# Decode attention over a KV cache: eight value blocks sent as 112 + 8 + 8 partitions instead of 128

## The chip, the cores and the metric

The kernel runs on one core of one Trainium2 chip. The metric is the device time of one execution in microseconds. Runs of the kernel before mostly agree within 0.3%. Times inside a profile count from the first instruction of the profiled run (its "span", 1 to 3 us shorter than the measured time).

## The reference, cut to what matters

Two attention layers decode one token for four sequences; A attends to all 8192 keys, B to the last 2048.

```python
def _A_ref(x, k_cache, v_cache, wq, wo):     # B=4, Sq=1, D=512, Hq=32, Hkv=8, Sk=8192, Dh=128, bf16
    q = (x @ wq) ...                         # per head
    scores = einsum("bhqd,bhkd->bhqk", q, k) * Dh ** -0.5
    p = softmax(scores)
    o = einsum("bhqk,bhkd->bhqd", p, v)
    return o ... @ wo
# B is the same on k_cache[:, :, Sk - 2048:], v_cache[:, :, Sk - 2048:]
# ... (result: concatenate A and B)
```

All of it is reading: 184.56 MB come from HBM, and every cached key and value is used once.

## The kernel before

Work is cut into 40 units: 8 of pass B, then 32 of pass A, one for each sequence and KV head. A unit of A has a key block and a value block of 2 MB each. Partition p holds 64 consecutive keys, so one block is 128 rows of 16 KB, one row to a partition.

```python
    def kv_src(cache, u, q=None):
        ...
            ap = cache[un["b"], un["g0"]].rearrange("(p t) d -> p t d", p=128)
    ...
        K_sb = sb("K_sb", [128, NKS, NT, DH], BF16)      # NKS = 3 slots
        V_sb = sb("V_sb", [128, NVS, NT, DH], BF16)      # NVS = 4 slots
    ...
        def sp_V(u):
            waits = [("PV", (u - NVS) * NQ + NQ - 1)] if u >= NVS else []
            # ... (last unit: four column quarters; pass B: two halves of the columns)
            else:
                op("sp", dma(kv_dst(V_sb, u % NVS, u), kv_src(VC[units[u]["P"]], u)), waits=waits, inc=("V", u))
```

SyncE issues one key and one value block per unit as slots come free. TensorE transposes the keys (L308 in the profile), forms the scores (L339) and multiplies probabilities by values (L365, the consumer of the changed transfers).

## Time and profile before

| | before |
|---|---|
| time, median of the runs | 454.71 us (453.95 to 455.2, four runs) |
| HBM bytes, rate over the span | 184.56 MB, 408 GB/s |
| TensorE busy | 370.2 of 452.4 us |
| 16 KB row on one DMA engine | 0.613 us |
| 16 KB rows over 0.7 us, after 119 us of the span | 45 of 7936 |

From the page of the kernel before, the lines of the 40 slices for DMA (busy tenths) and for GB/s, and two queues with packets, MB and share of 16 engines' time.

```profile
DMA  8999999999999999999999999999999999999971
GB/s 354 397 412 419 445 404 423 415 419 423 409 421 423 430 420 431 420 427 424 426 426 426 424 429 422 430 419 430 422 429 423 427 425 424 424 425 424 427 325 77
...
q1 hardware_dynamic: 17040, 184.56, 97.1%
q8 instruction: 53, 0.87, 0.8%
```

The DMA engines are busy nearly all the time, and from 150 us of the span to near its end they move about 425 GB/s. Queue q1 carries the tensors. Queue q8 is the fetching of instructions: few bytes.

The chain that ended last, from the same page, with shares of the span:

```profile
## 4 chain that ended last, share of the span: by engine, by line
DMA 54%; PE 38%; issue 3%; DVE 2%; ACT 1%; POOL 0%; POOLq 0%
DMA K_sb<-in_A_k_cache_dram 30%; PE ps L308 20%; DMA V_sb<-in_A_v_cache_dram 18%; DMA W<-in_A_wq_dram 6%; PE ps L365 6%; PE ps L339 5%; PE ps L438 3%; PE ps L254 2%; ACT KT_sb L317 1%; PE ps L728 1%; DVE KT_sb L316 1%; DVE M L456 1%; DVE Dt L494 0%; DVE xo_sb L553 0%; ACT PT L505 0%
```

The list of waits, before: who waited for whom, total us, times, longest.

```profile
...
PE ps L308 <- DMA K_sb<-in_A_k_cache_dram: 30.0, 19, 10.1
...
PE ps L365 <- DMA V_sb<-in_A_v_cache_dram: 9.0, 8, 2.3
...
```

TensorE waits for keys more than for values, in short gaps.

DMA issues, before: KB each, and the median time from issue to landing in us.

```profile
K_sb<-in_A_k_cache_dram SPq DMA_DIRECT2D x32, 2048.0 KB, 21.9
V_sb<-in_A_v_cache_dram SPq DMA_DIRECT2D x31, 2048.0 KB, 26.9
...
```

A block takes 8 x 0.613 = 4.9 us at the full rate, so 22 to 27 us from issue to landing means that about five blocks are queued.

The trace also holds every DMA packet, without the number of its engine. I chained each packet's end to the start that follows within a few ns, which rebuilds 16 engines (neighbours with equal times can be swapped in this, so I use it for groups, not for single engines over long times). About half of them land their last row near 436 us of the span, one at 440 us, the rest at 444.5 to 446 us. A fetch and the row behind it take 2.16 us, so a fetch costs its engine 2.16 - 0.61 = 1.55 us, and 53 fetches over eight engines are 53 x 1.55 / 8 = 10.3 us each. That is the skew the change aims at. That the fetches run on just eight engines is inferred from this sum and from their order, since the trace does not name the engines.

### The profile page before, as it was taken

The page shows a single profiled execution, that of the slowest core. Times are in us where ns is not written, and L with a number is a line of the kernel's source. Part 1 is how long each engine was busy: PE and PEld are TensorE (multiplying, and loading weights), DVE is VectorE, ACT ScalarE, POOL GpSimd, SP SyncE. Part 2 cuts the span into 40 slices and gives each one's busy share as a digit, 9 for nine tenths or more (in the row PEclk, how much of TensorE's full clock was granted, in tenths as well). Part 3 has the DMA queues.
Part 4 walks back from the last instruction along what each step waited for, and adds up shares of the span by engine and source line. Part 5 has one row for each costly group of instructions (what it writes and reads, how often), then busy time and mean ns, then how long its engine had stood idle before and what let it go on. Part 6 is the DMA issues. An engine that isn't in the chain of part 4 may idle for free.

```text
span 452.4 us, 14605 instructions
## 1 busy us (share of the span) xinstructions
PE 370.2 (82%) x6793; PEld 340.0 (75%) x6793; DVE 195.1 (43%) x449; ACT 178.0 (39%) x202; POOL 35.8 (8%) x93
## 2 busy tenths in 40 slices
PE   0682279999919998989978898878989789988997
PEld 0682279968818797888878888777979788888796
DVE  0351225748604453434434453444445344444362
ACT  1150214525503362534334453433444343345270
POOL 1100000100100110000000010001001000010010
PEclk9996655889958985968878896978868795698697
DMA  8999999999999999999999999999999999999971
GB/s 354 397 412 419 445 404 423 415 419 423 409 421 423 430 420 431 420 427 424 426 426 426 424 429 422 430 419 430 422 429 423 427 425 424 424 425 424 427 325 77
DMA packets 17181, 185.51 MB, mean 410 GB/s; under 512 B 1744, under 2 KB 2272, under 8 KB 4704
## 3 DMA queue, kind: packets, MB, share of 16 engines
q1 hardware_dynamic: 17040, 184.56, 97.1%
q8 instruction: 53, 0.87, 0.8%
q14 instruction: 8, 0.07, 0.0%
q0 software_dynamic: 64, 0.01, 0.0%
q10 hardware_dynamic: 16, 0.01, 0.0%
HBM read 184.56 MB, written 0.01 MB: 408 GB/s over the span
## 4 chain that ended last, share of the span: by engine, by line
DMA 54%; PE 38%; issue 3%; DVE 2%; ACT 1%; POOL 0%; POOLq 0%
DMA K_sb<-in_A_k_cache_dram 30%; PE ps L308 20%; DMA V_sb<-in_A_v_cache_dram 18%; DMA W<-in_A_wq_dram 6%; PE ps L365 6%; PE ps L339 5%; PE ps L438 3%; PE ps L254 2%; ACT KT_sb L317 1%; PE ps L728 1%; DVE KT_sb L316 1%; DVE M L456 1%; DVE Dt L494 0%; DVE xo_sb L553 0%; ACT PT L505 0%
## 5 line engine op out<-in xcount | busy, mean ns | idle before, releaser
L317 ACT ACTIVATE KT_sb<-ps 128x1024 bf16<-128x1024 bf16 x160 | 163.6, 1024 | 249.0 <-PE ps L308 248.7
L308 PE MATMUL ps<-identf,K_sb 128*128 128x128 f32 x1280 | 218.4, 329 | 41.9 <-DMA K_sb<-in_A_k_cache_dram 30.0
L308 PEld LDWEIGHTS ps<-identf,K_sb 128*128 128x128 f32 x1280 | 178.4, 170 | 56.1 <-DMA K_sb<-in_A_k_cache_dram 32.9
L316 DVE COPY KT_sb<-ps 128x512 int32<-128x512 int32 x160 | 110.4, 690 | 152.1 <-PE ps L308 151.4
L365 PE MATMUL ps<-PT,V_sb 128*128 128x4 bf16 (+1 forms) x2560 | 76.2, 165 | 9.3 <-DMA V_sb<-in_A_v_cache_dram 9.0
L365 PEld LDWEIGHTS ps<-PT,V_sb 128*128 128x128 bf16 x2560 | 70.8, 97 | 10.3 <-DMA V_sb<-in_A_v_cache_dram 10.2
L339 PEld LDWEIGHTS ps<-RQA,KT_sb 128*128 128x128 bf16 x2048 | 71.3, 99 | 3.7 <-ACT KT_sb L317 0.7
L339 PE MATMUL ps<-RQA,KT_sb 128*128 128x8 bf16 x2048 | 72.7, 167 | 1.1 <-issue 0.4
L526 POOL PARTITION_ALL_REDUCE LB<-L x40 | 17.4, 434 | 161.4 <-DVE L L517 161.4
L465 POOL PARTITION_ALL_REDUCE MB<-M x32 | 11.9, 373 | 172.7 <-DVE M L456 172.7
L456 DVE TENSOR_REDUCE M<-ps 128x4 f32<-128x256 f32 (+1 forms) x40 | 19.1, 478 | 12.6 <-PE ps L339 12.6
L543 DVE TENSOR_TENSOR OTg<-ps,RL 128x4 bf16<-128x4 f32 (+1 forms) x40 | 6.9, 174 | 40.5 <-PE ps L365 40.5
L517 DVE TENSOR_REDUCE L<-PT 128x4 f32<-128x256 bf16 (+1 forms) x40 | 21.9, 548 | 3.0 <-ACT PT L505 2.5
L339 PEld LDWEIGHTS ps<-RQB,KT_sb 128*128 128x128 bf16 x512 | 18.3, 100 | 2.1 <-ACT KT_sb L317 0.7
L339 PE MATMUL ps<-RQB,KT_sb 128*128 128x16 bf16 x512 | 18.8, 172 | 1.0 <-issue 0.5
L505 ACT ACTIVATE PT<-Dt 128x256 bf16<-128x256 f32 (+1 forms) x40 | 18.2, 454 | 3.6 <-DVE Dt L494 3.6
L438 PE MATMUL ps<-W,OL 128*4 128x512 bf16 x60 | 17.5, 436 | 0.1
L254 PE MATMUL ps<-xT,W 128*128 128x4 bf16 x256 | 7.5, 166 | 11.0 <-DMA W<-in_A_wq_dram 10.7
L254 PEld LDWEIGHTS ps<-xT,W 128*128 128x128 bf16 x256 | 7.1, 102 | 11.2 <-DMA W<-in_A_wq_dram 10.8
L494 DVE TENSOR_TENSOR Dt<-ps,MB 128x256 f32<-128x256 f32 x32 | 13.3, 415 | 0.5 <-POOL MB L465 0.5
L233 PE MATMUL ps<-ident,xo_sb 4*128 4x4 bf16 x8 | 0.6, 170 | 14.8 <-POOL identf L567 14.8
L233 PEld LDWEIGHTS ps<-ident,xo_sb 4*128 4x128 bf16 x8 | 0.4, 112 | 14.8 <-issue 14.7
(42 smaller groups left out, 63.5 us busy)
## 6 DMA issues: line engine op xcount, KB each, us to landing
K_sb<-in_A_k_cache_dram SPq DMA_DIRECT2D x32, 2048.0 KB, 21.9
V_sb<-in_A_v_cache_dram SPq DMA_DIRECT2D x31, 2048.0 KB, 26.9
K_sb<-in_B_k_cache_dram SPq DMA_DIRECT2D x16, 1024.0 KB, 18.8
V_sb<-in_B_v_cache_dram SPq DMA_DIRECT2D x16, 1024.0 KB, 22.1
W<-in_B_wq_dram SPq DMA_DIRECT2D x1, 4096.0 KB, 13.2
W<-in_B_wo_dram SPq DMA_DIRECT2D x1, 4096.0 KB, 34.3
W<-in_A_wq_dram SPq DMA_DIRECT2D x1, 4096.0 KB, 29.4
W<-in_A_wo_dram SPq DMA_DIRECT2D x1, 3584.0 KB, 32.7
```

Of the source, the lines that this page charges most:

```text
L254: ins = pe.matmul(out=bk[:, hl * Bn:(hl + 1) * Bn], lhsT=W1wq[:, c, hq * DH:(hq + 1) * DH], rhs=xT[:, P, c, :], start=(c == 0), stop=(c == ...
L308: ins = pe.transpose(out=bkf[:, pi * 128:(pi + 1) * 128], in_=K_sbf[:, slot, t0:t0 + 2, :].rearrange("p t d -> p (t d)"), identity=identf[ ...
L316: return e.tensor_copy(out=KT_sb.bitcast(I32)[:, tj % NKT, :], in_=bkf.bitcast(I32)[:, :])
L317: return e.activation(out=KT_sb[:, tj % NKT, :], in_=bk[:, :], func=ACTF.Copy)
L339: ins = pe.matmul(out=stb[:, t * CPT:(t + 2) * CPT], lhsT=ktv[:, pi, :, e], rhs=rhs, start=(e == 0), stop=(e == 1))
L365: ins = pe.matmul(out=otb[:, s * CPT:(s + 1) * CPT], lhsT=V_sb[:, vs, t, :], rhs=pt_cols(u, t * CPT, CPT), start=(j == 0), stop=(j == J - 1))
L438: ins = pe.matmul(out=opb[0:Bn, 0:D], lhsT=lhsT, rhs=wo_view[:, hq0 // REP + i // REP, i % REP, :], start=(first and i == 0), stop=(last a ...
L456: return dve.tensor_reduce(out=M1[:, 0:NC].rearrange("p (s h) -> p s h", h=CPT), in_=stb[:, 0:NT * CPT].rearrange("p (s j h) -> p s h j", ...
L494: return dve.tensor_tensor(out=Dt[:, 0:NT * CPT].rearrange("p (s j h) -> p s j h", s=S, h=CPT), in0=stb[:, 0:NT * CPT].rearrange("p (s j h ...
L505: return act.activation(out=PT[:, u % NPT, 0:NW], in_=Dt[:, 0:NW], func=ACTF.Exp, scale=scale)
L517: return dve.tensor_reduce(out=L1[:, 0:NC].rearrange("p (s h) -> p s h", h=CPT), in_=PT[:, u % NPT, 0:NT * CPT].rearrange("p (s j h) -> p ...
L526: return pool.partition_all_reduce(LB[:, 0:NC], L1[:, 0:NC], channels=128, reduce_op=ReduceOp.add)
```

## The change

Its intent: give the engines that fetch nothing two more rows in eight blocks, and so let all sixteen end together.

```diff
-        DMA_KEYS = ("K", "Kh", "V", "Vh", "VL", ...
+        DMA_KEYS = ("K", "Kh", "V", "Vh", "Vp", "VL", ...
...
+        PB, PX = DH - 16, 8
+
+        def sp_V_uneven(u, waits):
+            src, dst = kv_src(VC[0], u), kv_dst(V_sb, u % NVS, u)
+            for n, (p0, p1) in enumerate(((0, PB), (PB, PB + PX), (PB + PX, DH))):
+                op("sp", dma(dst[p0:p1], src[p0:p1]), waits=waits if n == 0 else [],
+                   inc=("V", u) if p1 == DH else ("Vp", u, n))
...
+            elif (u - NU_B) % Bn == 0 and u > NU_B or u == L - 1:
+                sp_V_uneven(u, waits)
             else:
```

More of the change, by code (lines that the diff above doesn't have):

```diff
@@ L174, in sem_of @@
                 return sem_k[key[1] % NKS]
-            if t in ("V", "Vh"):
+            if t in ("V", "Vh", "Vp"):
                 return sem_v[key[1] % NVS]
@@ L194, in sem_of @@
             }[t]
-        DMA_KEYS = ("K", "Kh", "V", "Vh", "VL", "x", "out", "W1", "W2", "mk")
+        DMA_KEYS = ("K", "Kh", "V", "Vh", "Vp", "VL", "x", "out", "W1", "W2", "mk")
         plan = {e: [] for e in ("sp", "pe", "act", "dve", "pool")}
```

## The prediction

> **What bounds it now.** The DMA engines. The page shows queue q1 at 97.1% of 16 engines' span; the stretch table gives a DMA share of 1.00 to 1.02 from 30 to 430 us at 420 to 426 GB/s, while PE is busy 42 to 46 of every 50 us. In the list of waits PE idles 30.0 us for K and 9.0 us for V of pass A. The chain of waits is DMA 54%, PE 38%.
>
> **Why the change exists.** A 16 KB packet of q1 takes 0.613 us (26.7 GB/s). I rebuilt the 16 engines from the trace by chaining each packet's end to the next one's start. The 53 instruction packets (q8, 16 KB, 1.07 us) recur on eight engines in turn; a fetch and the row after it take 2.16 us, so a fetch costs its engine 1.55 us: 53 x 1.55 / 8 = 10.3 us each. Eight engines land their last rows near 436 us of the span, the other eight at 444.5 to 446 us: a skew of about 9.5 us. [...]
>
> **What the change does.** SP gets 16 more issues of about 0.43 us, off the chain. The order on PE, DVE, ACT and POOL stays. [...] Eight blocks shift 8 x 0.613 = 4.9 us from the late half to the early half; the skew becomes about 0. If rows kept their 0.613 us, the last landing would come 4.9 us earlier. PE has little idle after 421.9 us, but its last waits for K (406 and 416 us) would move too: about 4.5 us of gain, 450 us.
>
> **Why I doubt it.** The rows go to the same SBUF partitions. [...] Add 4.9 us of extra rows, subtract 9.5 us of slack: +24 to +34 us. The 112-partition piece [...] perhaps 0 to 3 us a block. No trace here has such a transfer[...].
>
> **Numbers.** Predicted 480 us, range 449 to 512[...]. Faster by over 2%: 0.02; within 2%: 0.30; slower: 0.68.
>
> **What would show it.** [...] 16 KB packets of 1.2 to 3 us around the eight uneven blocks; GB/s dips below 420 there; issue to landing of V and K longer than 26.9 and 21.9 us; PE waits for K and V grow by tens of us. [...] packets stay 0.61 us, the skew vanishes, waits for K shrink by 4 to 5 us.
>
> **What would make it wrong.** [...] fetches on the lower eight (then +4.9 us); fewer engines used; buffering that hides short collisions (only 5 to 20 us slower).

Marked passages are cut, here and below, because they rest on a relation between engines and partitions that no trace or run shows. The forecast's sum came to +24 to +34 us. Its first term, the cost of slow rows in the two small pieces, was about +29 to +39 us, an estimate. The range had two humps, about 450 us if rows keep their time and 475 to 510 us if they slow down. Of the two lists of signs, the first is for rows that slow down, the second for rows that don't. That the small pieces run on the early half was assumed. "Low" (or "lower", "lowest") engines in these texts are those that the small pieces run on, "upper" ones the others; the trace gives engines no numbers.

## More of the kernel before

Busy time by stretch of the span, before; the last three columns are the TensorE clock, the share of DMA engine time and GB/s.

```profile
core 0: us, PE busy (x) PEld busy (x) DVE busy (x) ACT busy (x) POOL busy (x), PEclk, DMA share, GB/s
140.00:168.00 28.00, 26.98 (x512) 23.82 (x510) 13.34 (x32) 13.32 (x16) 2.42 (x6) 0.94 1.01 425
168.00:190.00 22.00, 19.63 (x336) 17.63 (x335) 9.92 (x25) 9.24 (x11) 1.82 (x5) 0.77 1.01 426
190.00:216.00 26.00, 22.83 (x446) 22.19 (x445) 10.14 (x23) 11.02 (x13) 2.20 (x6) 0.79 1.01 425
216.00:240.00 24.00, 21.43 (x361) 19.48 (x360) 11.38 (x27) 10.32 (x13) 1.61 (x4) 0.80 1.00 424
240.00:266.00 26.00, 23.16 (x459) 21.55 (x457) 11.83 (x29) 11.60 (x13) 2.14 (x6) 0.87 1.01 427
```

## The result, and the profile after

The changed kernel takes 560.07 us in the median of four runs (551.45 to 563.51), 454.71 us before. The ratio is 1.220, 95% interval 1.207 to 1.233. Ratios here are the mean time of one kernel's fast runs over that of the other's in the same rounds, so not quite the ratio of the medians quoted. Two of the four runs (562.01 and 563.51) were classed slow, being over 1.5% above the fastest; the profiled one, 558.12 us, was fast, and the cost is far larger than that spread. The change costs 105 us between the medians, and about 100 us between the means of fast runs (554.8 against 454.6).

The same lines of the page, after:

```profile
DMA  8999999999999999999999999889989997998940
GB/s 345 418 414 437 412 418 419 426 407 425 428 423 283 268 425 392 201 345 426 304 219 379 399 286 277 328 336 284 327 298 373 248 376 286 386 229 299 238 139 13
...
q1 hardware_dynamic: 17168, 184.56, 93.3%
q8 instruction: 53, 0.87, 0.7%
```

The 40 slices show the change at a glance. Up to its first uneven block the rate is that of before. Then come dips to 201 to 300 GB/s, about one for each block. The DMA busy tenths hardly fall at the first dips: the packets take longer, and a packet under way counts as busy. Multiplied out, the packets of q1 fill 0.971 x 452.4 = 439 us of each engine before and 0.933 x 556.4 = 519 us after. So about 80 of the 104 us by which the span grew are longer packets; the other 24 us are time in which an engine had no packet of q1, mostly late in the run (from 360 to 520 us the DMA share is 0.92 to 0.94), and were not looked into. The page has 17309 packets instead of 17181. The 128 added ones are 16 small transfers with 8 completion packets of 4 bytes each, where a whole block has 16: one for each engine, as I read it, so the small pieces do run on eight engines.

```profile
## 4 chain that ended last, share of the span: by engine, by line
DMA 70%; PE 23%; issue 3%; DVE 2%; ACT 1%; SPq 0%; POOL 0%; POOLq 0%
DMA V_sb<-in_A_v_cache_dram 61%; PE ps L308 10%; DMA W<-in_A_wq_dram 5%; PE ps L365 5%; DMA K_sb<-in_A_k_cache_dram 4%; PE ps L339 3%; PE ps L438 2%; PE ps L254 1%; ACT KT_sb L317 1%; DVE KT_sb L316 1%; PE ps L728 1%; DVE M L456 1%; DVE Dt L494 1%; SPq L598 0%; ACT PT L505 0%
```

The chain is now 61% value transfers. The waits of TensorE, after:

```profile
...
PE ps L308 <- DMA K_sb<-in_A_k_cache_dram: 62.3, 16, 10.1
...
PE ps L365 <- DMA V_sb<-in_A_v_cache_dram: 60.2, 19, 5.9
...
```

Waits for keys and for values both grow, together by (62.3 + 60.2) - (30.0 + 9.0) = 83.5 us. So the untouched key transfers suffer too. The granted TensorE clock fell as well, from 0.810 to 0.717 in the profiled runs. It is not what makes the dips: there the DMA engines have packets all the time, and it is the packets that take longer. The stretches, after, cut at the first two dips:

```profile
core 0: us, PE busy (x) PEld busy (x) DVE busy (x) ACT busy (x) POOL busy (x), PEclk, DMA share, GB/s
140.00:168.00 28.00, 27.39 (x488) 23.26 (x485) 11.65 (x30) 11.82 (x13) 2.09 (x6) 0.84 1.00 424
168.00:190.00 22.00, 12.83 (x213) 11.57 (x210) 7.53 (x16) 7.67 (x9) 1.55 (x4) 0.69 1.01 246
190.00:216.00 26.00, 21.57 (x412) 19.67 (x413) 9.57 (x23) 9.57 (x11) 1.60 (x4) 0.80 1.01 419
216.00:240.00 24.00, 14.07 (x203) 12.96 (x200) 6.71 (x15) 5.86 (x8) 1.17 (x3) 0.60 1.01 246
240.00:266.00 26.00, 19.81 (x329) 17.71 (x328) 8.72 (x23) 8.34 (x10) 1.60 (x4) 0.70 1.00 409
```

In the two bad stretches the DMA share is 1.01, against 1.01 and 1.00 before, but 246 GB/s move instead of 426 and 424. Worked out from these lines, (426 - 246) x 22 us / 426 = 9 us are lost in the first dip and (424 - 246) x 24 / 424 = 10 us in the second, of the 104 / 8 = 13 us that a block costs in the profiled run.

```profile
K_sb<-in_A_k_cache_dram SPq DMA_DIRECT2D x32, 2048.0 KB, 28.9
...
V_sb<-in_A_v_cache_dram SPq DMA_DIRECT2D x23, 2048.0 KB, 35.2
...
V_sb<-in_A_v_cache_dram SPq DMA_DIRECT2D x8, 1792.0 KB
...
V_sb<-in_A_v_cache_dram SPq DMA_DIRECT2D x16, 128.0 KB
```

Landing takes 28.9 us for keys and 35.2 us for whole value blocks, which were not changed themselves.

In the rebuilt packets, 2237 of the 7936 rows of 16 KB take over 0.7 us, most of them 1.0 to 1.4 us and some over 2. In the first dip, rows of the 112-partition transfer, of the key block ahead of it and of the one behind it mostly take about 1.1 to 1.5 us, on every engine. The order matters here. The first engines enter the 112-partition transfer (a run of seven rows) at 171.1 us of the span, and rows turn slow at that moment on all engines, those still reading the key block ahead included. The first row of a small piece starts only at 179.2 us. So in this dip the 112-partition transfer alone slowed every engine for 8 us.

### The profile page after: what moved, and what is told of

It reads as the page before. It is cut to its first block, busy times and chain, and to the rows that moved or that the text cites. A ratio compares the mean times of both kernels' runs of the same rounds, so it can differ in the third digit from the quotient of the medians.

```text
span 556.4 us, 14621 instructions
## 1 busy us (share of the span) xinstructions
PE 391.9 (70%) x6793; PEld 355.6 (64%) x6793; DVE 195.4 (35%) x449; ACT 178.0 (32%) x202; POOL 35.6 (6%) x93
## 2 busy tenths in 40 slices
DMA packets 17309, 185.52 MB, mean 333 GB/s; under 512 B 1872, under 2 KB 2400, under 8 KB 4832
## 4 chain that ended last, share of the span: by engine, by line
DMA 70%; PE 23%; issue 3%; DVE 2%; ACT 1%; SPq 0%; POOL 0%; POOLq 0%
DMA V_sb<-in_A_v_cache_dram 61%; PE ps L308 10%; DMA W<-in_A_wq_dram 5%; PE ps L365 5%; DMA K_sb<-in_A_k_cache_dram 4%; PE ps L339 3%; PE ps L438 2%; PE ps L254 1%; ACT KT_sb L317 1%; DVE KT_sb L316 1%; PE ps L728 1%; DVE M L456 1%; DVE Dt L494 1%; SPq L598 0%; ACT PT L505 0%
## 5 line engine op out<-in xcount | busy, mean ns | idle before, releaser
L308 PE MATMUL ps<-identf,K_sb 128*128 128x128 f32 x1280 | 230.9, 343 | 73.6 <-DMA K_sb<-in_A_k_cache_dram 62.3
L308 PEld LDWEIGHTS ps<-identf,K_sb 128*128 128x128 f32 x1280 | 190.1, 179 | 88.8 <-DMA K_sb<-in_A_k_cache_dram 64.6
L365 PE MATMUL ps<-PT,V_sb 128*128 128x4 bf16 (+1 forms) x2560 | 77.5, 166 | 60.4 <-DMA V_sb<-in_A_v_cache_dram 60.2
L365 PEld LDWEIGHTS ps<-PT,V_sb 128*128 128x128 bf16 x2560 | 72.1, 100 | 62.3 <-DMA V_sb<-in_A_v_cache_dram 62.1
L438 PE MATMUL ps<-W,OL 128*4 128x512 bf16 x60 | 23.2, 550 | 0.0
L413 DVE CAST OL<-ps 32x16 bf16<-32x16 f32 (+1 forms) x36 | 6.5, 182 | 44.5 <-PE ps L405 44.1
L438 PEld LDWEIGHTS ps<-W,OL 128*4 128x4 bf16 x60 | 5.5, 104 | 10.4 <-issue 8.5
## 6 DMA issues: line engine op xcount, KB each, us to landing
K_sb<-in_A_k_cache_dram SPq DMA_DIRECT2D x32, 2048.0 KB, 28.9
V_sb<-in_A_v_cache_dram SPq DMA_DIRECT2D x23, 2048.0 KB, 35.2
```

The costliest lines, as they stand in the source:

```text
L308: ins = pe.transpose(out=bkf[:, pi * 128:(pi + 1) * 128], in_=K_sbf[:, slot, t0:t0 + 2, :].rearrange("p t d -> p (t d)"), identity=identf[ ...
L365: ins = pe.matmul(out=otb[:, s * CPT:(s + 1) * CPT], lhsT=V_sb[:, vs, t, :], rhs=pt_cols(u, t * CPT, CPT), start=(j == 0), stop=(j == J - 1))
L438: ins = pe.matmul(out=opb[0:Bn, 0:D], lhsT=lhsT, rhs=wo_view[:, hq0 // REP + i // REP, i % REP, :], start=(first and i == 0), stop=(last a ...
```

## The experiments

Three theories were set against each other. P: the partitions written in SBUF (the on-chip memory) decide. H: the reads from HBM collide, because the rows read together are other ones. B: unequal bytes and small transfers cost the time. Later P was split: L (only the engines of the pieces and a few others slow down) and G (all do). Where the expectations have P double a row's time (from 0.613 us, or 0.38 us for 10 KB), and for its +15 to +25 us in e5, they give the author's estimate; no run had shown it.

### e1: 112 + 16, no imbalance

```diff
-            for n, (p0, p1) in enumerate(((0, PB), (PB, PB + PX), (PB + PX, DH))):
+            for n, (p0, p1) in enumerate(((0, PB), (PB, DH))):
```

> The eight blocks go as 112 partitions and one transfer of 16 partitions, so every engine carries 7 + 1 = 8 rows and nothing is uneven. Theory P [...]: [...] most of the cost stays, 510 to 560 us, rows of 1.2 us and more. Theory H (HBM reads: the addresses read together collide): also 510 to 560. Theory B (the 9-against-7 imbalance and the small pieces cost the time): 454 to 460 us.

Measured: 549.2 us, one run, correct (before, on the same chip: 455.11). Each of the two transfers of a block has 16 completion packets (128 more than before in all), so it runs on all engines and a block gives each eight rows again; 94 us of the cost stay. Theory B falls as the main cause. What the two 8-row pieces add is not resolved: the two fast runs of the changed kernel lie 2 and 9 us above this single run, whose state is unknown. Nor does e1 alone clear its 16-partition piece. Its trace does for the first dip: rows turn slow on all engines at 170.9 us of the span, as the first engines enter the 112-partition transfer, and the first row of the other piece starts at 179.1 us.

### e2 and e3: other addresses on the read side

```diff
 e2: one transfer of 128 partitions, source rows 28 KB apart
+            src = bass.AP(tensor=base.tensor, offset=base.offset, ap=[[NT * DH * 7 // 4, 128], [1, NT * DH]])
+            op("sp", dma(dst, src), waits=waits, inc=("V", u))
 e3: 112 + 8 + 8 as in the change, source rows 64 KB apart
+                src = bass.AP(tensor=base.tensor, offset=base.offset + p0 * NT * DH * 4,
+                              ap=[[NT * DH * 4, p1 - p0], [1, NT * DH]])
```

> The eight blocks go as one transfer of 128 partitions, but the rows are read from HBM at a pitch of 28 KB[...] (wrong values on purpose). Theory P: the write side is as before, 450 to 458 us. Theory H: the read side is like the changed kernel's, 500 to 560 us. Theory B: 454.

> The three pieces 112 + 8 + 8 as in the change, but the rows are read at a pitch of 64 KB (wrong values on purpose). Theory P: the read side does not matter, 550 to 565 us as the changed kernel. Theory H: another set of addresses, so another time, by 20 us or more either way. Theory B: 550 to 565.

Measured: 454.78 us for e2 and 559.91 us for e3, one run each, wrong values in both. The rate in the slices, e2 first and then e3:

```profile
GB/s 345 404 413 418 442 409 417 422 418 422 410 421 427 425 424 426 425 425 426 424 430 422 430 422 427 427 422 421 433 421 427 425 427 424 425 429 421 425 316 63
```

```profile
GB/s 345 422 413 436 413 418 419 424 409 423 430 422 269 293 430 373 203 389 427 276 208 387 422 213 244 337 383 263 272 333 371 253 318 297 385 242 308 258 149 17
```

The scattered read with the whole write leaves no dip; the split write with a different read has the dips of the change. Slow rows (over 0.7 us) are 45 in e2, as before, and 2597 in e3. H is out for the read patterns tried. (e3 says nothing against B, which expected the same time.)

### e4: two halves of 64 partitions

```diff
-            for n, (p0, p1) in enumerate(((0, PB), (PB, PB + PX), (PB + PX, DH))):
+            for n, (p0, p1) in enumerate(((0, DH // 2), (DH // 2, DH))):
```

> The eight blocks go as two transfers of 64 partitions, 0 to 63 and 64 to 127: 4 + 4 = 8 rows on each engine, 16 KB rows. Theory P: [...] rows take about 1.2 us and a block 9.8 instead of 4.9 us: 8 x 4.9 = 39 us more, 480 to 500 us. Theory H: [...] 454 to 460 us. Theory B: balanced, 454 to 458 us.

Measured: 549.7 us, one run, correct. Theory P had the direction, but 39 us were expected and 95 came, 11.8 us a block. The rows do take about twice as long (mostly 1.05 to 1.3 us in the first dip), as P expected. What P missed is how many: 2591 slow rows are 2591 / 8 / 16 = 20 per block on each engine, where a block has only 8. The key and value blocks next to it in the queue are slow as well.

### e5, e6, e7: the same extra pieces to different partitions

All value blocks go whole here. Behind the same eight blocks, two extra pieces of 8 partitions with 10 KB rows go to a tile that nobody reads. Only the destination partitions differ.

```diff
+            op("sp", dma(kv_dst(V_sb, u % NVS, u), src), waits=waits, inc=("V", u))
+            for n in range(2):
+                a, st = DSTS[n]
+                op("sp", dma(SCR[a:a + 7 * st + 1:st, :, :], src[DH - 16 + 8 * n:DH - 8 + 8 * n, 0:40, :]), ...
 e5: DSTS = [(112, 1), (120, 1)]   # 112..119, 120..127
 e6: DSTS = [(0, 4), (32, 4)]      # 0, 4, ..., 28 and 32, 36, ..., 60
 e7: DSTS = [(64, 4), (96, 4)]     # 64, 68, ..., 92 and 96, 100, ..., 124
```

> Every V block goes whole, as before; behind the same eight blocks come two extra pieces of 8 partitions, 10 KB a row, into a tile that nobody reads, on partitions 112-119 and 120-127 (correct values). [...] Each low engine carries 16 rows of 0.38 us = 6.1 us more, inside the slack of about 9.5 us if the low engines are the early half. Theory P[...]: [...] +15 to +25 us in all. Theory B (more bytes on eight engines): 0 to +6 us. The 10 KB packets also mark the low engines in the trace, which shows whether those or the others fetch instructions.

> As the previous run, with the same source rows, sizes, engines and count, but the pieces go to partitions 0, 4, ..., 28 and 32, 36, ..., 60[...]. Theory P: no collision, 10 KB rows of 0.38 us, 450 to 458 us. Theory B: the same time as the previous run.

> As the previous run, but to partitions 64, 68, ..., 92 and 96, 100, ..., 124[...]. Theory P: [...] the rows take twice as long and the upper engines lose 16 x 0.38 = 6 us: 458 to 466 us; far more if a collision holds up others. Theory B: the same time as the two others.

| run | median | ratio to before, 95% interval | median 10 KB packet, the slowest |
|---|---|---|---|
| e5, consecutive partitions | 474.24 us | 1.042 (1.040 to 1.045) | 0.584, 1.187 us |
| e6, 0 to 60 in steps of four | 459.32 us | 1.010 (1.007 to 1.012) | 0.385, 0.392 us |
| e7, 64 to 124 in steps of four | 472.85 us | 1.040 (1.038 to 1.043) | 0.577, 0.921 us (*) |

(Four runs each; 454.94 us before, same chip. (*) Left out are two packets of 1.032 us that follow an 8 KB instruction fetch on their engine.) e5 lies within what P expected; e7 lies above its range (458 to 466 us), and e6 just above its own (450 to 458 us). The stretch of the first extra pieces in e6, then in e7 (columns as above):

```profile
176.00:184.00 8.00, 7.81 (x100) 6.98 (x101) 4.11 (x11) 3.37 (x4) 0.43 (x1) 0.68 1.01 425
```

```profile
176.00:184.00 8.00, 7.49 (x85) 6.57 (x86) 3.63 (x8) 3.38 (x4) 0.80 (x2) 0.60 0.98 306
```

Same bytes, same source rows, same number of issues and of packets (17437 in both): 425 GB/s against 306. The choice of partitions alone decides. In e6 none of the 128 extra packets takes over 0.392 us, while in e5 and e7 95 and 86 of 128 take over 0.42 us. Spreading a piece in steps of four partitions (e7) is not what helps, since it cost as much as eight partitions in a row (e5). I had picked the three sets on an assumption about which engine writes which partitions, and it named the harmless one. That is no proof of it: the trace does not name the engines, so what the partitions of e6 have that the others lack is not shown.

The 4.4 us of e6 need another reason. With 10 KB packets as markers, the trace shows the eight engines of the pieces apart: at the block near 416 us of the span five of them pass within 2.2 us, and the other three come 3, 7 and 9 us behind the fifth. So two of the eight clearly belong to the late half. The third, 3 us behind, lies between the halves; it seems to be one of the four that e10 (below) loads.

### e8 and e9: how far the slowing reaches

```diff
 e8: 2 partitions in a piece, DSTS = [(64, 4), (96, 4)]   # 64, 68 and 96, 100
 e9: 8 partitions in a piece, DSTS = [(4, 4), (5, 4)]     # 4, 8, ..., 32 and 5, 9, ..., 33
```

> Extra pieces of only 2 partitions (64 and 68, then 96 and 100)[...]; 4 rows of 10 KB per block in all. Theory L [...]: at most two further engines see slow rows, and the time stays within 2 us of the kernel before. Theory G [...]: rows of all 16 engines around each piece exceed 0.65 us; the pieces take some 1.5 to 3 us a block, and at about 60% of the rate each block loses 1 us or so: +4 to +12 us.

> Pieces of 8 partitions to 4, 8, ..., 32 and 5, 9, ..., 33[...]. Theory L: only the low eight slow down, [...] +5 to +10 us. Theory G: all sixteen slow down and the time is that of the run [...], +15 to +20 us.

Measured, four runs each (before 454.35 us): e8 460.72 us, ratio 1.014 (1.012 to 1.016); e9 475.43 us, ratio 1.048 (1.044 to 1.051). In e8 there are only 32 extra rows of 10 KB in the whole run, with two completion packets a piece, so on two engines each; 255 rows of 16 KB take over 0.65 us, 193 more than the 62 of e6: six slow rows for each extra one. Around the first pieces, 13 rows have their middle in the same 0.6 us (178.0 to 178.6 us of the span), and each takes over 0.65 us. One engine can't have two such rows there, so at least 13 of 16 engines are slowed by two pieces of two rows. Both results are on the side of G. e9 cost no less than e7, which is the run that its expectation compares it with: 21 us, a little over G's 15 to 20. The kept trace of e9 shows whom it slowed: at seven of its eight blocks, 14 to 16 rows of 16 KB that take over 0.65 us are under way at one moment, against at most 5 in the kernel before. The pieces run on eight engines, so engines that carry no piece are slowed too. e9 also writes low partitions as e6 does, so it is not the half of the partitions that made e6 harmless.

### e10: as e6, but on four engines only

```diff
-                op("sp", dma(SCR[a:a + 7 * st + 1:st, :, :], src[DH - 16 + 8 * n:DH - 8 + 8 * n, 0:40, :]), ...
+                op("sp", dma(SCR[a:a + 3 * st + 1:st, :, :], src[DH - 16 + 8 * n:DH - 12 + 8 * n, 0:40, :]), ...
```

> As the run [...], but with 4 partitions (0, 4, 8, 12 and 32, 36, 40, 44), so only the lowest four engines carry 6.1 us more. If those four are all in the early half[...], and three of the lowest eight are in the late half, this run costs nothing: 454 to 456 us against 459.3 us for eight. If the lowest eight are alike, it costs the same as that run, +4 us.

Measured: 454.69 us, ratio 1.0016 (0.9992 to 1.0040). A piece has four completion packets here (128 packets more than before in all, 64 of them rows), so it runs on four engines. They take 16 x 0.385 = 6.2 us more each at no cost in time, so they have slack. At the block near 416 us, one of these four runs 2.7 us behind the last of the other three. The eight engines of e6 do not all have it: e6 cost 4.4 us. The eight that the pieces run on are therefore the wrong set to load, whatever the partitions.

### e11: one uneven block

```diff
-            elif (u - NU_B) % Bn == 0 and u > NU_B or u == L - 1:
+            elif u == NU_B + 4 * Bn:
```

> The change at one block in the middle instead of eight. If every uneven block costs the same by itself, +13 us (a eighth of 105 us): 466 to 470 us. If the cost builds up over blocks, less, 456 to 462 us.

Measured: 466.77 us, ratio 1.027 (1.026 to 1.029), so 12.4 us for one block.

```profile
GB/s 348 403 412 418 432 419 416 420 419 423 407 431 426 422 427 421 424 424 427 430 424 427 426 426 394 208 241 426 427 423 426 426 424 424 427 427 421 426 329 62
```

One dip and full rate after it. Eight times 12.4 us is 99 us, which is about all that the eight blocks cost between fast runs (100 us): the cost is per block and builds up little.

## Why the prediction was wrong

- **What bounds the kernel: right.** DMA bounded it, and the loss of GB/s is the loss of time.
- **The direction, and the reason for doubt: right.** The probability of slower was 0.68, because the rows still go to the same partitions. The signs named for slow rows came: row times (forecast 1.2 to 3 us, mostly 1.0 to 1.4 us measured), dips, longer landing, waits longer by tens of us. e2, e3 and the e5 to e7 set show that the destination decides.
- **The size: wrong. The step that failed is the cost of the 112-partition piece.** The prediction charged the two small pieces (about 29 to 39 us over eight blocks), and gave the 112-partition piece "perhaps 0 to 3 us a block". The second, a guess, was mis-sized. With the pieces gone but 112 + 16 kept (e1), 94 us remain, 11.8 us a block, and the traces show the 112-partition transfer slowing all engines 8 us before any other piece starts. The first term was not absurd by itself: pieces of 10 KB rows on the same partitions behind whole blocks (e5) cost 19.3 us, inside the 15 to 25 us that the same estimate gave. But the terms do not add up: beside a 112-partition transfer the pieces cost some 2 to 9 us more.
- **Why that term was set so small: the model was local.** It let a small piece delay the engines that carry it and few others. The runs show slow rows on at least 13 of 16 engines from two pieces of two rows (e8), and 20 slow rows an engine for a block of 8 (e4). In the first dip after the change, rows are slow (median of every 2 us over 0.64 us) from 171 to 193 us of the span, though seven rows of 0.613 us are only 4.3 us of work for an engine. I take this for the time from the first engine's entry into the transfer to the last one's leaving it, with other blocks in between; that is inferred.
- **That the small pieces run on the early half: wrong.** e10 shows that the four engines it loads have slack, but of the eight that carry the pieces of e6, two are late. If the 16 KB pieces run on the same eight, they load late engines too. Had the partitions not mattered, these two would have got 8 x 0.613 = 4.9 us more on top of their fetches; the 4.4 us of e6 for 6.2 us of extra rows suggests a loss, not the 4.5 us gain of the "450 us" branch. This is worked out, not run: no transfer here moves rows off the late engines without slow rows.
- **What stays open.** Why engines that carry no piece slow down too was not found. Nor is it shown what sets the harmless partitions of e6 and e10 apart from those of e5, e7, e8 and e9, or which engine takes which rows of a 112-partition transfer and why they run slow. No version beat the kernel before. The fetches that the late engines carry might be made to shrink instead, which was not tried.

## What to carry to other kernels

Here a block load on all 128 partitions ran at full rate (0.613 us a row), and each of the three ways to split it by partitions cost 94 us or more over eight blocks (112 + 8 + 8, 112 + 16, 64 + 64). So before splitting or rebalancing such a load, try one block, which shows the whole cost (12.4 us here), and vary the partitions of a piece (1.0% against 4.0% in e6 and e7). With many transfers in flight, a badly placed piece was paid by its neighbours in the queue as well (20 slow rows an engine for a block of 8 in e4). Read GB/s beside the DMA busy share, since in the first two dips the share stays at 1.0 while the rate falls from 425 to 246 GB/s.
